# Turning q and k of three batches by DMA transposes, and spreading the value means by VectorE, in a fused attention and gated feed-forward kernel

## Chip, cores, metric

The kernel runs on one core of one Trainium2 chip. The metric is the device time of one execution in microseconds, as the median over several executions. The profile is of one more execution, recorded by the hardware profiler. Its span runs 1 to 3 us under the device time. Only fast runs are compared; a run counts as slow when it is over 1.5% above the fastest of the same kernel on its chip.

## The reference, cut to what matters

```python
B, H, S, D = 4, 8, 768, 64;  block, window = 32, 16
k_sum = k.reshape(B, H, 24, 32, D).max(axis=3)       # block maxima of the keys
v_sum = v.reshape(B, H, 24, 32, D).mean(axis=3)      # block means of the values
scores = concat(banded q k^T (|i - j| < 16), q k_sum^T + log 32)   # scaled by 1/8
x = softmax(scores) @ concat(v, v_sum)               # then (tokens, 512)
out = x + sigmoid(x w_res) * ((gelu(x w_gate) * (x w_val)) w_out)
```

Scores need q and k with the head dimension on the partitions, so q and k have to be turned. The weighted sum needs the values with the tokens on the partitions, and the block means beside them in every window.

## The kernel before

The work is cut into eight units, two per batch. An even unit of batch b and an odd one each run the feed-forward stage of 384 tokens. In the tail of each unit the attention of the next unit is computed. An odd unit also prepares the next batch in its gate/value stage. Only batch 0 is prepared ahead of all this. A **gate/value stage** is the loop of twelve `fo_step`, a **tail** is everything after it up to the next unit's first gate product, and an **odd unit** is one stage and one tail.

```python
def load_qk(src, b, parts, name):            # token p*8+j of a head -> partition p, 1 KB pieces
    ...
        nc.gpsimd.dma_start(out=t[...].rearrange("p h j d -> p h (j d)"),
                            in_=src[b, ...].rearrange("h (p j) d -> p h (j d)", j=PJ))

def v_loads(b):                              # 12 overlapping windows of 96 tokens, 128-byte pieces
    for t in range(NT):
        r0, r1, src = v_window(b, t)
        nc.gpsimd.dma_start(out=vext[b % 2][r0:r1, t, :, 0:D], in_=src)

def turn_pair(src, hp, pool, tag):           # 16 small TensorE transposes
    ...
def k_step(b, hp, pool, tag):
    tp = turn_pair(k_sb[b], hp, pool, tag)
    nc.scalar.copy(kw[:, 1:NT - 1, 0:BAND]..., src)         # ScalarE copies the windows
    nc.vector.tensor_copy(...); nc.vector.tensor_copy(...)  # VectorE the two edges
    nc.vector.tensor_reduce(out=ks..., in_=kw[...], axis=X, op=ALU.max)
    nc.vector.tensor_copy(kw[:, :, BAND:BAND + NB], ks.unsqueeze(1).to_broadcast([128, NT, NB]))

def vsum_grp(b, pool, tag):                  # block means: 12 matmuls, one copy, four small DMAs
    ...
    nc.vector.tensor_copy(vpart[:], vs[:])
    for g in range(4):
        nc.sync.dma_start(out=vsum[b % 2][96 + 6 * g:102 + 6 * g, :], in_=vpart[32 * g:32 * g + 6, :])

def vsum_bc(b, lo, hi, eng):                 # the means spread to windows lo..hi
    eng.tensor_copy(vext[b % 2][96:128, lo:hi, :, 0:D], <vsum broadcast>)

def fo_step(st, gvT, fo):                    # 8 matmuls, gelu on ScalarE, product on VectorE
    ...
    nc.scalar.activation(ge[:], g[:, 0:TU], AF.Gelu)
    nc.vector.tensor_mul(gvT[:, fo, :], ge[:], vv[:, 0:TU])   # frees vv's PSUM bank (4 banks)
...
for u in range(NU):
    b, half = u // 2, u % 2
    nb = b + 1
    if half == 0 and nb < B:
        k_sb[nb] = load_qk(k, nb, 1, "k_sb"); q_sb[nb] = load_qk(q, nb, 1, "q_sb"); v_loads(nb)
    for fo in range(FO):
        fo_step(st, gvT, fo)
        if half == 1 and nb < B:
            if fo == 1:
                vsum_grp(nb, ps_t, "t")
                vsum_bc(nb, 0, 4, nc.gpsimd); vsum_bc(nb, 4, 8, nc.gpsimd); vsum_bc(nb, 8, NT, nc.gpsimd)
            elif 2 <= fo < 6:  k_step(nb, fo - 2, ps_t, "t")
            elif 6 <= fo < 10: q_step(nb, fo - 6, ps_t, "t")
    ...                                      # tail: scores, weighted sums, residual gate, output
```

Each engine runs its instructions in program order. GpSimd issues all loads, SyncE the outputs and the small means DMAs.

The softmax here doesn't subtract the row's maximum and nothing guards it: scores larger than these inputs give would overflow.

## Time and profile before

| kernel before | value |
|---|---|
| device time, median | 306.96 us (305.46 to 307.67) |
| span of the profiled run | 304.4 us |
| PE busy | 272.4 us, 89% |
| odd units (stage + tail) of batches 1, 2, 3 being prepared | 42.4, 39.3, 38.0 us |
| even units in between | 29.7, 29.8 us |

The unit times are differences of the starts of the first gate product of each unit in the timeline.

From the page of the kernel before: the busy times, the packet count, and the chain of waits (its share of the span by engine).

```profile
PE 272.4 (89%) x2563; PEld 149.6 (49%) x2586; DVE 170.5 (56%) x375; ACT 137.7 (45%) x204; POOL 80.4 (26%) x104
...
DMA packets 54987, 22.88 MB, mean 75 GB/s; under 512 B 37480, under 2 KB 51888, under 8 KB 54960
...
PE 65%; DMA 14%; POOL 7%; DVE 6%; issue 5%; ACT 1%; POOLq 0%; DVEq 0%
```

The kernel is bound by TensorE, with 32 us in which TensorE is idle.

The timeline shows one source of it: while GpSimd spreads the means (5.57 us), VectorE's copy of the block maxima, 0.23 us at its best, takes up to 1.91 us, and the product that frees PSUM stands behind it. The GpSimd lines also show the order: the next batch's loads are issued only after the spread.

```profile
145.29 5.57 POOL L222 COPY vext_107<-vsum_109 32x2048 bf16<-32x2048 bf16 x3 [47.45 <-DMA vsum_109<-vpart]
...
149.06 1.91 DVE L192 COPY kW_2_93<-ks 128x288 bf16<-128x288 bf16 x1
...
150.81 0.77 POOL L82 DMA_DIRECT2D k_sb<-in_k_dram  x1
150.88 0.53 DVE L282 TENSOR_TENSOR gvT<-ge,vv 128x384 bf16<-128x384 f32 x1
```

### The profile page before, as it was taken

Reading aid. Unit: us, or ns where it says so; the run is one execution under the profiler, and the core shown is the slowest. Engines: PE = TensorE matmul, PEld = TensorE weight load, DVE = VectorE, ACT = ScalarE, POOL = GpSimd, SP = SyncE. Lnnn points to the kernel's source line nnn. Section 1 sums busy time; section 2 is a strip of 40 time slices with the busy share of each in tenths; the row PEclk is TensorE's granted clock in tenths of the full one; section 3 lists DMA queues with packets and bytes.
Section 4 is the critical chain, followed back from the end, with each engine's and each line's share of the span. In section 5 each row is a group of like instructions: output and inputs, shape, how many; then the busy total and the mean of one; then the engine's idle time right before and its main releaser. Section 6 shows DMA issues by size and latency. Waiting matters only on the chain.

```text
span 304.4 us, 6192 instructions
## 1 busy us (share of the span) xinstructions
PE 272.4 (89%) x2563; PEld 149.6 (49%) x2586; DVE 170.5 (56%) x375; ACT 137.7 (45%) x204; POOL 80.4 (26%) x104
## 2 busy tenths in 40 slices
PE   1665999988699999999799999999799999999993
PEld 0622565544354566455355556455354556455641
DVE  3445544673953854476933854386944854475433
ACT  2642536432466533644456533643566433643310
POOL 7976673320954000000974000000700000000000
PEclk9999599997999999999979999999999999999999
DMA  6999999991199910011099910011000110010001
GB/s 100 168 98 186 197 206 207 162 164 33 10 200 114 84 61 2 0 71 37 3 176 131 90 69 2 2 51 56 4 2 0 56 49 2 1 71 34 2 34 69
DMA packets 54987, 22.88 MB, mean 75 GB/s; under 512 B 37480, under 2 KB 51888, under 8 KB 54960
## 3 DMA queue, kind: packets, MB, share of 16 engines
q0 software_dynamic: 51360, 16.13, 81.3%
q1 hardware_dynamic: 3600, 6.37, 6.3%
q8 instruction: 20, 0.33, 0.4%
q14 instruction: 7, 0.06, 0.1%
HBM read 32.24 MB, written 6.29 MB: 127 GB/s over the span
## 4 chain that ended last, share of the span: by engine, by line
PE 65%; DMA 14%; POOL 7%; DVE 6%; issue 5%; ACT 1%; POOLq 0%; DVEq 0%
PE f L298 18%; PE g L274 16%; PE vv L278 15%; DMA vext_108<-in_v_dram 8%; PE r L288 6%; DMA w_val<-in_moe_w_val_dram 3%; DVE ks L188 3%; DMA vext_107<-in_v_dram 3%; PE tp L172 3%; PE ao L250 2%; POOL vext_107 L97 2%; PE s L232 2%; PE xp L261 2%; DVE gvT L282 2%; POOL vext_107 L222 1%
## 5 line engine op out<-in xcount | busy, mean ns | idle before, releaser
L282 DVE TENSOR_TENSOR gvT<-ge,vv 128x384 bf16<-128x384 f32 x96 | 52.9, 551 | 63.3 <-PE vv L278 63.2
L274 PE MATMUL g<-xT,w_gate 128*128 128x384 bf16 x384 | 82.3, 334 | 0.0
L281 ACT ACTIVATE ge<-g 128x384 f32<-128x384 f32 x96 | 47.1, 491 | 75.9 <-DVE gvT L282 41.3
L278 PE MATMUL vv<-xT,w_val 128*128 128x384 bf16 x384 | 80.1, 332 | 0.0
L298 PE MATMUL f<-w_out,gvT 128*128 128x512 bf16 x274 | 65.3, 379 | 1.5 <-issue 1.1
L278 PEld LDWEIGHTS <-w_val 128*128 128x128 bf16 x384 | 38.2, 100 | 26.9 <-issue 3.2
L274 PEld LDWEIGHTS <-w_gate 128*128 128x128 bf16 x384 | 35.7, 99 | 25.2 <-issue 4.2
L236 ACT ACTIVATE P<-s,bias_t 128x768 bf16<-128x768 f32 x32 | 28.9, 903 | 35.0 <-PE s L232 35.0
L298 PEld LDWEIGHTS <-gvT 128*128 128x128 bf16 x288 | 27.3, 98 | 31.0
L239 DVE TENSOR_TENSOR P<-P,maskt 128x768 bf16<-128x768 bf16 x32 | 17.7, 554 | 22.0 <-ACT P L236 22.0
L222 POOL COPY vext_108<-vsum_110 32x2048 bf16<-32x2048 bf16 x6 | 11.1, 1895 | 58.5 <-DMA vsum_110<-vpart 58.5
L288 PE MATMUL r<-w_res,xT 128*128 128x512 bf16 x88 | 24.4, 381 | 0.4
L97 POOL DMA_DIRECT2D vext_108<-in_v_dram x24 | 18.2, 770 | 18.9 <-DMA w_out<-in_moe_w_out_dram 4.7
L222 POOL COPY vext_107<-vsum_109 32x2048 bf16<-32x2048 bf16 (+1 forms) x4 | 8.3, 2108 | 47.5 <-DMA vsum_109<-vpart 47.4
L303 DVE SCALAR_TENSOR_TENSOR th<-th,f 128x512 f32<-128x512 f32 x24 | 16.3, 680 | 7.0 <-PE f L298 7.0
L97 POOL DMA_DIRECT2D vext_107<-in_v_dram x24 | 18.1, 762 | 6.5 <-PE g L274 3.3
L172 PE MATMUL tp<-ident,k_sb 96*64 96x96 bf16 x256 | 10.1, 232 | 10.6 <-DMA k_sb<-in_k_dram 6.5
L256 DVE TENSOR_TENSOR xn<-ao,rz 128x384 bf16<-128x384 f32 x32 | 17.9, 558 | 1.1
L291 ACT ACTIVATE th<-r 128x512 f32<-128x512 f32 x24 | 14.3, 594 | 8.8 <-PE r L288 8.4
L305 DVE SCALAR_TENSOR_TENSOR o<-th,xn 128x512 f32<-128x512 f32 x24 | 16.6, 692 | 0.8
L172 PE MATMUL tp<-ident,q_sb 96*64 96x96 bf16 x256 | 10.1, 232 | 6.7 <-DMA q_sb<-in_q_dram 3.0
L250 PEld LDWEIGHTS <-P 128*64 128x64 bf16 x384 | 8.9, 113 | 14.4 <-DVE P L239 5.9
(151 smaller groups left out, 220.2 us busy)
## 6 DMA issues: line engine op xcount, KB each, us to landing
out_dram<-o SPq DMA_DIRECT2D x24, 256.0 KB
k_sb<-in_k_dram POOLq DMA_DIRECT2D x3, 768.0 KB, 7.5
q_sb<-in_q_dram POOLq DMA_DIRECT2D x3, 768.0 KB, 10.6
vext_107<-in_v_dram POOLq DMA_DIRECT2D x20, 96.0 KB, 7.8
vext_108<-in_v_dram POOLq DMA_DIRECT2D x20, 96.0 KB, 10.9
w_gate<-in_moe_w_gate_dram POOLq DMA_DIRECT2D x6, 256.0 KB, 8.8
w_val<-in_moe_w_val_dram POOLq DMA_DIRECT2D x6, 256.0 KB, 9.3
w_out<-in_moe_w_out_dram POOLq DMA_DIRECT2D x3, 512.0 KB, 14.2
```

Of the source, the lines that this page charges most:

```text
L97: nc.gpsimd.dma_start(out=vext[b % 2][r0:r1, t, :, 0:D], in_=src)
L172: nc.tensor.transpose(tp[hh * 64:hh * 64 + 64, j, :], src[:, 2 * hp + hh, j, :], ident[0:PP, 0:PP])
L222: eng.tensor_copy(vext[b % 2][96:128, lo:hi, :, 0:D], src)
L236: nc.scalar.activation(P.rearrange("p a t q -> p a (t q)"), s[:, :, 0:TU], AF.Exp, scale=scale, bias=bias_t[:])
L239: nc.vector.tensor_mul(Pf, Pf, maskt.unsqueeze(1).to_broadcast([128, 2 * HT, QT]))
L256: nc.vector.tensor_mul(xn, ao[:, :, :, 0:D], rz.to_broadcast([128, NSUB, 2, D]))
L274: nc.tensor.matmul(g[:, 0:TU], w_gate[:, ko, fs], st["xT"][:, ko, :], start=(ko == 0), stop=(ko == KO - 1))
L278: nc.tensor.matmul(vv[:, 0:TU], w_val[:, ko, fs], st["xT"][:, ko, :], start=(ko == 0), stop=(ko == KO - 1))
L281: nc.scalar.activation(ge[:], g[:, 0:TU], AF.Gelu)
L282: nc.vector.tensor_mul(gvT[:, fo, :], ge[:], vv[:, 0:TU])
L288: nc.tensor.matmul(r[:], st["xT"][:, ko, ss], w_res[:, ko, :], start=(ko == 0), stop=(ko == KO - 1))
L298: nc.tensor.matmul(st["f"][:], gvT[:, fo, ss], w_out[:, fo, :], start=(fo == 0), stop=(fo == FO - 1))
```

## The change

The intent is to take q's and k's turning off TensorE, ScalarE and VectorE for batches 1 to 3. Their tokens are loaded with tokens on the partitions, and one DMA transpose each turns all of k and all of q. Values are loaded first. The means are spread by VectorE in four pieces, after the gate/value products 4 to 7, and the block maxima follow products 8 to 11.

```diff
+    k_nat = const.tile([BAND, NT, DM], BF16, name="k_nat")
+    q_nat = const.tile([128, NQ, DM], BF16, name="q_nat")
+    def load_nat(b):                       # 12 windows of k, 6 blocks of q, 128-byte pieces
+        for t in range(NT): ... nc.gpsimd.dma_start(out=k_nat[r0:r0 + hi - lo, t]..., in_=k[b, :, lo:hi, :]...)
+        for c in range(NQ): ... nc.gpsimd.dma_start(out=q_nat[:, c]..., in_=q[b, ...]...)
+
+    def turn_all(b):
+        nc.sync.dma_start_transpose(out=kW[b % 2].rearrange("d t g k -> d (t g) k")[:, :, 0:BAND],
+                                    in_=k_nat.rearrange("p t f -> p (t f)"))
+        nc.sync.dma_start_transpose(out=qT[b % 2].rearrange("d c g k -> d (c g) k"),
+                                    in_=q_nat.rearrange("p c f -> p (c f)"))
 ... (kW and qT become one tile per batch parity; k_blocks = the maxima part of k_step)
             if half == 0 and nb < B:
-                k_sb[nb] = load_qk(k, nb, 1, "k_sb")
-                q_sb[nb] = load_qk(q, nb, 1, "q_sb")
                 v_loads(nb)
+                load_nat(nb)
 ...
                     if fo == 1:
                         vsum_grp(nb, ps_t, "t")
-                        vsum_bc(nb, 0, 4, nc.gpsimd)
-                        vsum_bc(nb, 4, 8, nc.gpsimd)
-                        vsum_bc(nb, 8, NT, nc.gpsimd)
-                    elif 2 <= fo < 2 + NP:
-                        k_step(nb, fo - 2, ps_t, "t")
-                    elif 2 + NP <= fo < 2 + 2 * NP:
-                        q_step(nb, fo - 2 - NP, ps_t, "t")
+                    elif 4 <= fo < 8:
+                        vsum_bc(nb, 3 * (fo - 4), 3 * (fo - 3), nc.vector)
+                    elif 8 <= fo:
+                        k_blocks(nb, fo - 8)
 ...
             end_step(u, st, 2)
+            if half == 0 and nb < B:
+                turn_all(nb)
```

More of the change, by code (lines that the diff above doesn't have):

```diff
@@ L46 @@
     BAND = QT + 2 * WIN
+    NQ = S // 128
     PJ = 8
@@ L51 @@
     wpool = ctx.enter_context(tc.tile_pool(name="wpool", bufs=1))
-    qk = ctx.enter_context(tc.tile_pool(name="qk", bufs=2))
+    qk = ctx.enter_context(tc.tile_pool(name="qk", bufs=1))
     work = ctx.enter_context(tc.tile_pool(name="work", bufs=3))
@@ L67 @@
     warm = const.tile([128, 512], BF16, name="warm")
-    kW = [[const.tile([128, NT, 128], BF16, name=f"kW{i}_{p}") for p in range(NP)] for i in range(2)]
-    qT = [[const.tile([128, S], BF16, name=f"qT{i}_{p}") for p in range(NP)] for i in range(2)]
+    kW = [const.tile([128, NT, NP, 128], BF16, name=f"kW{i}") for i in range(2)]
+    qT = [const.tile([128, NQ, NP, 128], BF16, name=f"qT{i}") for i in range(2)]
+    k_nat = const.tile([BAND, NT, DM], BF16, name="k_nat")
+    q_nat = const.tile([128, NQ, DM], BF16, name="q_nat")
     vext = [const.tile([128, NT, H, D + 1], BF16, name=f"vext{i}") for i in range(2)]
@@ L99 @@
     k_sb, q_sb = {}, {}
+    def load_nat(b):
+        for t in range(NT):
+            lo, hi = max(0, t * QT - WIN), min(S, t * QT + QT + WIN)
+            r0 = lo - (t * QT - WIN)
+            nc.gpsimd.dma_start(out=k_nat[r0:r0 + hi - lo, t].rearrange("p (h d) -> p h d", d=D),
+                                in_=k[b, :, lo:hi, :].rearrange("h p d -> p h d"))
+        for c in range(NQ):
+            nc.gpsimd.dma_start(out=q_nat[:, c].rearrange("p (h d) -> p h d", d=D),
+                                in_=q[b, :, c * 128:(c + 1) * 128, :].rearrange("h p d -> p h d"))
+    def turn_all(b):
[3 more added lines that the diff above has]
+                                    in_=q_nat.rearrange("p c f -> p (c f)"))
     with tc.manual_schedule():
@@ L148 @@
         for p in range(NP):
-            nc.vector.memset(kW[0][p][:, 0, 0:WIN], 0.0)
-            nc.vector.memset(kW[0][p][:, NT - 1, BAND - WIN:BAND], 0.0)
-            nc.vector.memset(kW[0][p][:, :, BAND + NB:128], 0.0)
+            nc.vector.memset(kW[0][:, 0, p, 0:WIN], 0.0)
+            nc.vector.memset(kW[0][:, NT - 1, p, BAND - WIN:BAND], 0.0)
+            nc.vector.memset(kW[0][:, :, p, BAND + NB:128], 0.0)
         nc.vector.memset(warm[:], 0.0)
@@ L174, in turn_pair, with k_blocks @@
             return tp
+        def k_blocks(b, hp):
+            kw = kW[b % 2][:, :, hp]
+            ks = work.tile([128, NB], BF16, tag="ks", name="ks")
+            nc.vector.tensor_reduce(
+                out=ks.rearrange("d (t n) -> d t n", n=2),
+                in_=kw[:, :, WIN:WIN + QT].rearrange("d t (n w) -> d t n w", w=BLK),
+                axis=mybir.AxisListType.X, op=ALU.max)
+            nc.vector.tensor_copy(kw[:, :, BAND:BAND + NB], ks.unsqueeze(1).to_broadcast([128, NT, NB]))
         def k_step(b, hp, pool, tag):
             tp = turn_pair(k_sb[b], hp, pool, tag)
-            kw = kW[b % 2][hp]
+            kw = kW[b % 2][:, :, hp]
             src = bass.AP(tensor=tp.tensor, offset=tp[:, 0, 6:7].offset,
@@ L186, in k_step @@
                                   tp[:, :, PP - 10:PP].rearrange("d j p -> d p j"))
-            ks = work.tile([128, NB], BF16, tag="ks", name="ks")
-            nc.vector.tensor_reduce(
-                out=ks.rearrange("d (t n) -> d t n", n=2),
-                in_=kw[:, :, WIN:WIN + QT].rearrange("d t (n w) -> d t n w", w=BLK),
-                axis=mybir.AxisListType.X, op=ALU.max)
-            nc.vector.tensor_copy(kw[:, :, BAND:BAND + NB], ks.unsqueeze(1).to_broadcast([128, NT, NB]))
+            k_blocks(b, hp)
         def q_step(b, hp, pool, tag):
             tp = turn_pair(q_sb[b], hp, pool, tag)
-            nc.scalar.copy(qT[b % 2][hp].rearrange("d (p j) -> d p j", j=PJ),
-                           tp.rearrange("d j p -> d p j"))
+            nc.scalar.copy(qT[b % 2][:, :, hp].rearrange("d c (p j) -> d c p j", j=PJ),
+                           tp.rearrange("d j (c p) -> d c p j", c=NQ))
         def vsum_mm(b, pool, tag):
@@ L226, in s_step @@
             s = ps_s.tile([128, 2, 512], F32, tag="s", name="s")
-            kw, qt = kW[b % 2][hp], qT[b % 2][hp]
+            kw, qt = kW[b % 2], qT[b % 2]
             for t in range(HT):
@@ L231, in s_step @@
                     ps = slice(hh * 64, hh * 64 + 64)
-                    nc.tensor.matmul(s[:, hh, t * QT:(t + 1) * QT], kw[ps, tt, :],
-                                     qt[ps, tt * QT:(tt + 1) * QT], start=True, stop=True,
+                    nc.tensor.matmul(s[:, hh, t * QT:(t + 1) * QT], kw[ps, tt, hp, :],
+                                     qt[ps, tt // 2, hp, (tt % 2) * QT:(tt % 2 + 1) * QT], start=True, stop=True,
                                      skip_group_check=True)
@@ L334 @@
         own_keys(bgrp, 3)
+        nc.vector.memset(k_nat[0:32, 0], 0.0)
+        nc.vector.memset(k_nat[64:96, NT - 1], 0.0)
         for p in range(NP):
-            nc.vector.memset(kW[1][p][:, 0, 0:WIN], 0.0)
-            nc.vector.memset(kW[1][p][:, NT - 1, BAND - WIN:BAND], 0.0)
-            nc.vector.memset(kW[1][p][:, :, BAND + NB:128], 0.0)
+            nc.vector.memset(kW[1][:, 0, p, 0:WIN], 0.0)
+            nc.vector.memset(kW[1][:, NT - 1, p, BAND - WIN:BAND], 0.0)
+            nc.vector.memset(kW[1][:, :, p, BAND + NB:128], 0.0)
         for u in range(NU):
```

## The prediction

> **What bounds the kernel now.** The page gives PE 272.4 of 304.4 us; the chain of waits is PE 65%, DMA 14%. By windows, the gate/value stage of an even unit (107 to 124 us) is 17.0 us with PE busy throughout; in an odd unit, which also prepares the next batch, it is 25.7 us (136.6 to 162.3) and 25.2 (205.8 to 231). The first one (64.4 to 93) is 28.6: the timeline shows PE waiting for the last value windows until 70.0. So preparation costs about 8 us three times, plus some 3 us once. In the timeline it is 128 small transposes (8 bursts of about 0.53 us), their PSUM waits behind ScalarE's 0.96 us copies, and VectorE's 0.95 us maxima and 0.23 to 1.9 us copies, the slow ones beside GpSimd's 1.9 us copies.
>
> **Removed.** Per batch: those transposes, 8 ScalarE copies (0.8 and 0.96), 8 edge copies (0.23), GpSimd's 5.6 us of spreading. **Added.** VectorE spreads four pieces, an estimate of 0.5 us each (its 32x3072 copy took 0.96). Left on VectorE in the stage: 12 x 0.55 + 0.7 + 2 + 4 x 1.25 = about 14 us, under PE's 16 to 17. If nothing waited, an odd stage would fall to about 17.5, the time to about 280.
>
> **What I expect instead: new waits.**
> 1. Packets. q and k came in 1 KB pieces: 1,536 per batch in about 7.4 us (208 per us in the trace). Token-major they are 128-byte pieces like v's, k with overlapping windows: 8,960 + 6,144, at v's rate (about 790 per us) some 19 us; with v 31 us a batch instead of 19.
> 2. Batch 1. Weights hold the DMA until about 50 us; then v to 62, k to 73, q to 81 or later. The transposes stand on SyncE in front of the four small block-mean DMAs, and its instructions go in order. VectorE reaches the first spread at about 72, and blocks, with gate/value products behind it, until q has landed, both transposes and the small DMAs are done: 85 to 97. About 10 us of VectorE work remain then. This stage ends near 95.5 at best, more likely 103 to 106, against 93.
> 3. Batches 2 and 3 have their data early, but transposes are issued only as the odd unit begins, and VectorE needs the means about 7 us later. Transposing 1.97 MB: the Trainium skill (Advanced Engine Details and Errata, X-Bar Transpose (TRN2)) expects 350 to 400 GB/s, an estimate of 5 to 6 us; as 7,680 rows of 256 bytes at v's packet rate it is about 10 us. No record of before shows a transpose. For batch 2 the v loads of batch 3 start at the same moment and compete (11 us of DMA). I estimate the means at 12 to 20 us for batch 2, 10 to 16 for batch 3: stages of 23 to 31 and 21 to 27 against 25.
>
> **Sum.** Against before: batch 1 +10, batch 2 +3, batch 3 -2: 307 + 11 = 318 us. Range 298 to 350, skewed up because the transposes' speed is unmeasured. Faster by over 2%: 0.18; within 2%: 0.24; slower by over 2%: 0.58.
>
> **Signs.** PE loses 384 transposes; its busy time falls by some 15 us, its idle time rises by more. VectorE's first spread waits for the block-mean DMA, longest in batch 1 (12 to 25 us), and SyncE's queue waits there for q's load. DMA packets under 512 B grow by about 45,000. Even units stay near 17 us, tails near 13.
>
> **Wrong if:** transposes take 5 us, even beside loads, with SyncE free at once: then 295 to 305. Transposes or their issue over 20 us per batch: 350 or more. Or q's and k's small packets go well faster than v's, so batch 1 hardly waits.

## More of the kernel before

The kernel before scattered from 300.8 to 309.6 us over all chips used.

The next lines are stretches of the kernel before: the stage of each of the three odd units. The columns are the stretch, its length, the busy time of PE, PEld, DVE, ACT and POOL, the granted clock, the mean DMA share and GB/s. (The DMA share adds up the times of packets that overlap, so it can exceed 1.)

```profile
64.50:93.00 28.50, 23.68 (x239) 12.57 (x235) 17.32 (x32) 12.43 (x21) 12.56 (x13) 0.94 0.86 99
136.60:162.10 25.50, 23.18 (x240) 12.56 (x237) 16.39 (x32) 12.46 (x21) 12.38 (x12) 0.93 0.54 83
205.70:229.80 24.10, 21.58 (x239) 11.93 (x236) 16.48 (x32) 12.36 (x21) 5.57 (x3) 1.00 0.05 16
```

An even unit's stage takes about 16 us. So the preparation inside an odd stage costs 8 to 10 us, and 12.6 in the first. All tails are 13.8 to 13.9 us.

## The result, and the profile after

The changed kernel takes 328.85 us in the median (328.32 to 330.35) against 307.31 of the kernel before on the same chip: a ratio of 1.0713, 95% interval 1.066 to 1.0766, slower. Ratios here are the mean time of one kernel's fast runs over the mean of the other's in the same rounds, so they are not quite the ratios of the medians quoted.

From the page of the changed kernel, the lines that answer to those of before.

```profile
PE 263.6 (80%) x2202; PEld 142.6 (43%) x2202; DVE 170.2 (52%) x365; ACT 118.2 (36%) x180; POOL 102.5 (31%) x143
...
DMA packets 119689, 29.82 MB, mean 91 GB/s; under 512 B 106792, under 2 KB 116592, under 8 KB 119664
...
PE 75%; DMA 10%; SPq 6%; ACT 3%; DVE 3%; issue 2%; POOL 1%; DVEq 0%; POOLq 0%
```

SyncE's queue (SPq) is new on the chain. Stages of the three odd units of the changed kernel (the tails, 13.8 to 14.4 us, are left out):

```profile
63.50:109.10 45.60, 19.61 (x112) 10.30 (x109) 13.79 (x23) 5.90 (x13) 32.60 (x42) 0.70 2.22 157
152.80:184.00 31.20, 19.78 (x111) 10.24 (x108) 14.01 (x24) 5.91 (x13) 16.79 (x22) 0.78 1.70 161
227.60:253.00 25.40, 19.02 (x111) 10.05 (x108) 13.27 (x22) 5.88 (x12) 0.00 (x0) 0.87 0.50 92
```

TensorE's work in a stage did fall, from about 23 to 19.5 us, and ScalarE's from 12.4 to 5.9. But the stages grew from 28.5, 25.5 and 24.1 us to 45.6, 31.2 and 25.4. With the tails the odd units take 59.5, 45.0 and 39.8 us: 17.1, 5.7 and 1.8 more than before. Their sum is 24.6, the spans differ by 24.0. So the loss is wholly in these three units.

What happens in the first one is told by SyncE's timeline and by VectorE's and TensorE's (start, duration, instruction; in brackets the idle time before it and what ended it). First SyncE of the changed kernel:

```profile
72.63 9.36 SPq L115 DMA_TRANSPOSE kW_92<-k_nat  x1
82.21 8.70 SPq L117 DMA_TRANSPOSE qT_94<-q_nat  x1
90.97 2.97 SPq L239 DMA_DIRECT2D vsum_100<-vpart  x4
...
155.47 8.09 SPq L115 DMA_TRANSPOSE kW_91<-k_nat  x1
163.84 3.72 SPq L117 DMA_TRANSPOSE qT_93<-q_nat  x1
167.68 2.85 SPq L239 DMA_DIRECT2D vsum_99<-vpart  x4
...
230.28 5.95 SPq L115 DMA_TRANSPOSE kW_92<-k_nat  x1
236.46 4.20 SPq L117 DMA_TRANSPOSE qT_94<-q_nat  x1
240.76 2.85 SPq L239 DMA_DIRECT2D vsum_100<-vpart  x4
```

Then VectorE and TensorE of the changed kernel in the first odd unit:

```profile
71.38 0.55 DVE L305 TENSOR_TENSOR gvT<-ge,vv 128x384 bf16<-128x384 f32 x1 [0.75 <-PE vv L301]
100.30 0.95 DVE L245 COPY vext_98<-vsum_100 32x1536 bf16<-32x1536 bf16 x1 [28.37 <-DMA vsum_100<-vpart]
```

```profile
75.10 0.81 PE L297 MATMUL g<-xT,w_gate 128*128 128x384 bf16 x4
101.90 1.44 PE L301 MATMUL vv<-xT,w_val 128*128 128x384 bf16 x4 [25.98 <-DVE gvT L305]
103.13 1.49 PE L297 MATMUL g<-xT,w_gate 128*128 128x384 bf16 x4
```

The chain is complete in these lines. SyncE issues k's transpose at 72.6 us, when k's last window has landed, and q's behind it. (q had landed at 77.1 us by the trace; its transpose waited for SyncE, which k's held until 82.0.) Only then, at 91.0, come the four small means DMAs, whose data was ready at about 68. VectorE has reached the first spread at 71.9 and sits 28.4 us. The products behind it don't free PSUM banks, so TensorE, after filling what was free, sits 26.0 us. Afterwards four matmuls start 1.23 to 1.28 us apart group by group instead of 0.65, until 107 us, where the granted clock is back. The Trainium skill ("TensorE: Matmul & The Clock Gate", section "What's actually happening") says that the array falls to half its clock after idling and regains it with sustained work. The mean granted clock of this stage is 0.70, and about 5 us run at half speed (101.9 to 107.2).

The means landed 36.8 us after the start of the first odd unit, 22.2 after that of the second, 17.2 after that of the third. VectorE wants them after about 8.4. In the last one no load runs, and the transposes alone do it: 5.95 and 4.20 us of SyncE, and 4 us for the means. In the first the same two take 9.36 and 8.70 us, and the means another 9.3. Why, the page doesn't say, but GpSimd's timeline shows that it issued twelve v loads of batch 2 from 72.6 to 88.8 us, during these transposes, and k loads of batch 3 from 165.5 us, into the wait for batch 2's means:

```profile
72.64 6.20 POOL L100 DMA_DIRECT2D vext_97<-in_v_dram  x8
...
165.54 9.04 POOL L108 DMA_DIRECT2D k_nat<-in_k_dram  x12 [10.25 <-DMA kW_91<-k_nat]
```

### The profile page after: what moved, and what is told of

Same layout as the page of the kernel before. It is cut to its first block, busy times and chain, and to the rows that moved or that the text cites. A ratio compares the mean times of both kernels' runs of the same rounds, so it can differ in the third digit from the quotient of the medians.

```text
span 328.4 us, 5481 instructions
## 1 busy us (share of the span) xinstructions
PE 263.6 (80%) x2202; PEld 142.6 (43%) x2202; DVE 170.2 (52%) x365; ACT 118.2 (36%) x180; POOL 102.5 (31%) x143
## 2 busy tenths in 40 slices
DMA packets 119689, 29.82 MB, mean 91 GB/s; under 512 B 106792, under 2 KB 116592, under 8 KB 119664
## 4 chain that ended last, share of the span: by engine, by line
PE 75%; DMA 10%; SPq 6%; ACT 3%; DVE 3%; issue 2%; POOL 1%; DVEq 0%; POOLq 0%
PE g L297 19%; PE vv L301 19%; PE f L321 18%; PE r L311 6%; DMA vext_97<-in_v_dram 4%; SPq L117 4%; PE ao L273 3%; DMA vsum_100<-vpart 3%; PE s L255 3%; PE xp L284 2%; DMA q_sb<-in_q_dram 2%; SPq L239 2%; DMA vsum_99<-vpart 2%; PE wp L342 1%; ACT qT_93 L219 1%
## 5 line engine op out<-in xcount | busy, mean ns | idle before, releaser
L301 PE MATMUL vv<-xT,w_val 128*128 128x384 bf16 x384 | 83.0, 341 | 43.8 <-DVE gvT L305 43.8
L297 PE MATMUL g<-xT,w_gate 128*128 128x384 bf16 x384 | 84.1, 340 | 0.0
L301 PEld LDWEIGHTS <-w_val 128*128 128x128 bf16 x384 | 38.9, 101 | 72.9 <-issue 50.4
L321 PE MATMUL f<-w_out,gvT 128*128 128x512 bf16 x288 | 68.4, 379 | 0.0
L297 PEld LDWEIGHTS <-w_gate 128*128 128x128 bf16 x384 | 38.5, 102 | 29.0 <-issue 8.2
L108 POOL DMA_DIRECT2D k_nat<-in_k_dram x36 | 27.2, 762 | 16.6 <-DMA kW_91<-k_nat 10.3
L245 DVE COPY vext_98<-vsum_100 32x1536 bf16<-32x1536 bf16 x8 | 7.6, 952 | 37.3 <-DMA vsum_100<-vpart 37.1
L262 DVE TENSOR_TENSOR P<-P,maskt 128x768 bf16<-128x768 bf16 x32 | 17.7, 553 | 16.8 <-ACT P L259 16.8
L100 POOL DMA_DIRECT2D vext_97<-in_v_dram x24 | 18.3, 784 | 7.3 <-DMA vext_97<-in_v_dram 6.5
L328 DVE SCALAR_TENSOR_TENSOR o<-th,xn 128x512 f32<-128x512 f32 x24 | 16.6, 692 | 0.8
L111 POOL DMA_DIRECT2D q_nat<-in_q_dram x18 | 15.8, 911 | 0.0
L277 DVE RECIPROCAL rz<-ao 128x6 f32<-128x6 f32 x32 | 6.2, 193 | 12.8 <-PE ao L273 12.8
## 6 DMA issues: line engine op xcount, KB each, us to landing
w_out<-in_moe_w_out_dram POOLq DMA_DIRECT2D x3, 512.0 KB, 13.8
```

The lines of the kernel that those rows point to most:

```text
L108: nc.gpsimd.dma_start(out=k_nat[r0:r0 + hi - lo, t].rearrange("p (h d) -> p h d", d=D), in_=k[b, :, lo:hi, :].rearrange("h p d -> p h d"))
L262: nc.vector.tensor_mul(Pf, Pf, maskt.unsqueeze(1).to_broadcast([128, 2 * HT, QT]))
L297: nc.tensor.matmul(g[:, 0:TU], w_gate[:, ko, fs], st["xT"][:, ko, :], start=(ko == 0), stop=(ko == KO - 1))
L301: nc.tensor.matmul(vv[:, 0:TU], w_val[:, ko, fs], st["xT"][:, ko, :], start=(ko == 0), stop=(ko == KO - 1))
L321: nc.tensor.matmul(st["f"][:], gvT[:, fo, ss], w_out[:, fo, :], start=(fo == 0), stop=(fo == FO - 1))
```

## The experiments

Theory A: the time is lost by order. VectorE waits, in order, for means that stand behind the transposes on SyncE. Theory A' is named in e4's expectation ("Theory A with contention") and tested by itself in e6, after the first four runs: A, and the waits are as long as they are because GpSimd's loads run ahead and compete with the transposes. Rival B: the small packets of q and k cost the time, wherever the transposes stand. Rival C: VectorE has too much work in the stage. All diffs are against the changed kernel unless said otherwise. All results below but one (e3, wrong in its values) compute the reference's result.

The table gives each odd unit's time in the profile (from its first gate product to that of the next unit), the median, and the ratio to the kernel before of the same rounds.

| run | odd units, us | median, us | ratio (95%) |
|---|---|---|---|
| before | 42.4, 39.3, 38.0 | 305.1 to 307.3 | 1 |
| changed | 59.5, 45.0, 39.8 | 328.85 | 1.0713 (1.066 to 1.0766) |
| e1 means first | 51.2, 35.7, 35.5 | 307.60 | 1.0087 (1.0048 to 1.0127) |
| e2 means by ScalarE | 51.5, 36.7, 36.6 | 310.24 | 1.0166 (1.0123 to 1.0209) |
| e3 no q and k loads | 43.7, 41.2, 39.7 | 311.93 | 1.0232 (1.0206 to 1.0258) |
| e4 spread by GpSimd | 39.4, 32.9, 34.7 | 293.08 | 0.9612 (0.957 to 0.9654) |
| e5 other part alone | 41.1, 36.9, 36.9 | 302.18 | 0.99 (0.9875 to 0.9926) |
| e6 GpSimd waits | 47.6, 39.8, 39.4 | 312.25 | 1.0311 (1.0187 to 1.0434) |
| e7 early transposes | 60.0, 34.7, 31.3 | 311.15 | 1.0276 (1.0113 to 1.044) |
| e8 e4 + early transposes | 39.2, 30.6, 30.6 | 285.31 | 0.9425 (0.9316 to 0.9534) |
| e9 e8, batch 1 on TensorE | 39.6, 30.6, 30.7 | 286.83 | 0.9474 (0.9364 to 0.9584) |
| e10 e11, two spreads | 46.1, 30.7, 30.6 | 295.02 | 0.9659 (0.9631 to 0.9688) |
| e11 e6 + early transposes | 42.9, 31.6, 31.4 | 296.12 | 0.9695 (0.967 to 0.972) |
| e12 e8, batch 1's means first | 43.7, 30.6, 30.7 | 290.72 | 0.9509 (0.9465 to 0.9554) |

e1 to e4, e6 to e9, and e10 to e12 with e5 shared a chip and its runs of the kernel before each time. The medians of before on these three chips lie within 0.7 us, so medians are set side by side across them.

The recorded verdicts, at 2% and from fast runs alone: changed and e3 slower; e1 and e5 the same; e4, e10, e11 and e12 faster; e2 and e6 to e9 unclear. For e6 to e9 the three fast runs of before are 305.1, 304.8 and 300.8 us, and the last one widens the interval. Against the mean of all seven, 305.1 us, their ratios would be 1.023, 1.020, 0.935 and 0.940.

### e1: the means DMAs ahead of the transposes

```diff
                         vsum_grp(nb, ps_t, "t")
+                        turn_all(nb)
 ...
-            if half == 0 and nb < B:
-                turn_all(nb)
```

> The changed kernel, with both transposes issued after the four block-mean DMAs on SyncE (in the odd unit, right after the group sums) instead of before them. Theory A (the time is lost because the block-mean DMAs stand behind the transposes in SyncE's order, and VectorE, which waits for the means in order, holds back the gate/value products): VectorE's first spread comes about 8.5 us after the odd unit's start in all three batches, its wait there is under 2 us; the later transposes then delay the block maxima and the next scores instead. Odd gate/value stages of about 30 (batch 1, data late), 23 and 20 us; about 303 us in all. Rival B (the 45,000 more small DMA packets of q and k cost the time wherever the transposes stand): still 320 us or more. Rival C (VectorE has too much work in the odd stage): unchanged within 5 us, 324 or more.

Measured: 307.60 us, ratio 1.0087. VectorE's first spread in batch 1:

```profile
74.80 0.95 DVE L245 COPY vext<-vsum 32x1536 bf16<-32x1536 bf16 x1 [2.97 <-DMA vsum<-vpart]
```

It waits 3.0 us there and 0.4 in batch 2, and the loss of the change is all but gone, as A says; B and C are 12 us or more off. A's figure of 303 was too low by 5 us. The first stage took 35.0 us, not 30: k's transpose took 9.66 us and q's 10.29, VectorE waited 8.9 us for the first maxima and TensorE 5.3 us for q. That pointed to the transposes being slow in batch 1 whatever stands behind them. GpSimd's v loads of batch 2 ran beside them here too, from 72.2 us.

### e2: the means DMAs issued by ScalarE

```diff
-            nc.sync.dma_start(out=vsum[b % 2]...
+            nc.scalar.dma_start(out=vsum[b % 2]...
```

> The changed kernel, with the four block-mean DMAs issued by ScalarE instead of SyncE; the transposes stay where they are. Theory A: the means no longer stand behind the transposes, VectorE's first spread comes about 9 us after the odd unit's start; batch 1 is still held by the late q and k (next scores at about 94 us instead of 109), batches 2 and 3 have stages of 18 to 19 us against 31 and 25; in all about 294 us, faster than the kernel before. ScalarE loses some 3 us per batch to issuing. Rival B (small packets): 320 or more. Rival C (VectorE's work): 324 or more.

Measured: 310.24 us, a miss by 16 us in its size, though again far under B and C. In batch 2 the first spread comes 13.9 us after the odd unit's start, not 9. ScalarE's and SyncE's lines of this run in the second odd unit say where it went:

```profile
147.09 8.21 SPq L115 DMA_TRANSPOSE kW<-k_nat  x1
149.04 5.19 ACTq L239 DMA_DIRECT2D vsum<-vpart  x4
154.33 0.87 ACT L304 ACTIVATE ge<-g 128x384 f32<-128x384 f32 x2 [7.08 <-DMA vsum<-vpart]
```

The four issues take ScalarE 5.19 us beside a transpose's issue, where the first odd unit's four, issued before any transpose, took 3.38. The gelu behind them waits 7.08 us, and with it the product and TensorE. A second queue didn't get the small DMAs past the transposes cheaply. What makes the issue slow is not shown.

### e3: q and k of batches 1 to 3 not loaded (wrong result on purpose)

```diff
                 v_loads(nb)
-                load_nat(nb)
 ...
-        nc.vector.memset(k_nat[0:32, 0], 0.0)
-        nc.vector.memset(k_nat[64:96, NT - 1], 0.0)
+        nc.vector.memset(k_nat[:], 0.0)
+        nc.vector.memset(q_nat[:], 0.0)
```

> Wrong result on purpose: q and k of batches 1 to 3 are not loaded (their tiles are zeroed once), the rest of the changed kernel is kept, so 45,000 small packets less and no wait for data. Theory A: only batch 1 gains, its transposes start at about 66 us instead of 72.6 and end sooner; the stages are 29 to 31, 31 and 25 us instead of 45, 31 and 25; 314 us in all (311 to 319). Rival B (the packets of q and k are the cost): back at the time of before or under it, 290 to 307. Rival C: 325 or more.

Measured: 311.93 us, within A's 311 to 319. With 45,312 fewer small load packets the kernel is still 2.3% slower than before, so B can't be the whole. The first odd unit gained 15.8 us. The second gained 3.8, which A had not expected: in the changed kernel k's and q's loads of batch 3 start when batch 2's k transpose ends (165.5 us) and share the DMA engines with q's transpose and the means, which then landed 7.3 us after their first issue instead of 4.1 here. The loads matter, then, through what they collide with.

### e4: the means spread by GpSimd, as before the change

```diff
                         vsum_grp(nb, ps_t, "t")
-                    elif 4 <= fo < 8:
-                        vsum_bc(nb, 3 * (fo - 4), 3 * (fo - 3), nc.vector)
+                        vsum_bc(nb, 0, 4, nc.gpsimd)
+                        vsum_bc(nb, 4, 8, nc.gpsimd)
+                        vsum_bc(nb, 8, NT, nc.gpsimd)
```

> The changed kernel, with the means spread by GpSimd in three pieces as before, the DMAs and transposes as changed. VectorE no longer waits for the means, and GpSimd, waiting for them in its order, issues the next batch's v loads only afterwards, so they do not compete with the transposes. Theory A with contention: the means land at about 90 us instead of 100 in batch 1, and 17 us after the odd unit's start in batches 2 and 3 (22 and 17 before); each transpose pair takes 6 + 4 us on SyncE; the values weighted by the scores wait for the spread by some 4 us; about 292 to 300 us in all. If competing loads are not what slows the transposes of batch 1 (9.4 and 8.7 us), these stay near 9 us. Rival B: 320 or more.

Measured: 293.08 us, 3.9% faster than the kernel before, in the expected 292 to 300. Every packet and both transposes of the change are still there, in the same order on SyncE. Means landed at 88.7 us instead of 100.3, and the transposes of batch 1 took SyncE 7.53 and 4.79 us instead of 9.36 and 8.70. So B falls. But this run changes two things at once: VectorE no longer blocks, and GpSimd's loads no longer run ahead. e6 parts them.

### e6: VectorE's spread kept, GpSimd made to wait for the means

```diff
+    hold = const.tile([128, 1], BF16, name="hold")
 ...
                         vsum_grp(nb, ps_t, "t")
+                        nc.gpsimd.tensor_copy(hold[96:128, :], vsum[nb % 2][96:128, 0:1])
```

> The changed kernel in everything, and in addition GpSimd copies one column of the means (32 elements) in the odd unit, so that it issues the next batch's loads only after the means have landed. VectorE still spreads and still waits behind the transposes. Theory A' (the prediction's mechanism is right and its size was off because GpSimd runs ahead with the next batch's loads, which slow the transposes and the small means DMAs in batches 1 and 2): the first spread comes at about 89 us instead of 100 in batch 1 and 17 to 18 us after the odd unit's start instead of 22 in batch 2, as in the run with GpSimd's spread; batch 3 is unchanged at 17; about 312 us in all, 16 less. If competing loads do not matter: 326 or more.

Measured: 312.25 us, as expected to 0.3 us. This is the run that shows why the loss was larger than predicted. One copy of 0.19 us on GpSimd takes 16.6 us off the medians (328.85 to 312.25) and 18.3 off the spans. These are not of the same rounds; the ratios to before, 1.0713 and 1.0311, give some 12 us, the second with an interval of 4 us to either side. SyncE and GpSimd of this run in the first odd unit, and VectorE's first spread in the second:

```profile
71.59 7.55 SPq L116 DMA_TRANSPOSE kW<-k_nat  x1
79.37 3.64 SPq L118 DMA_TRANSPOSE qT<-q_nat  x1
83.07 2.98 SPq L240 DMA_DIRECT2D vsum<-vpart  x4
```

```profile
87.24 0.19 POOL L379 COPY hold<-vsum 32x1 bf16<-32x1 bf16 x1 [15.42 <-DMA vsum<-vpart]
87.77 9.18 POOL L101 DMA_DIRECT2D vext<-in_v_dram  x12 [0.34 <-issue]
...
156.73 0.95 DVE L246 COPY vext<-vsum 32x1536 bf16<-32x1536 bf16 x1 [8.41 <-DMA vsum<-vpart]
```

Batch 2's v loads now start at 87.8 instead of 72.6 us, and the first spread comes at 87.2 instead of 100.3. The packet records tell it directly. A batch's transposes write 7,680 packets of 256 bytes. In the changed kernel's batch 1 these were spread over 20.5 us, with 9,061 packets of 128 bytes of loads in between them; here over 10.0 us, with 775. In the changed kernel's batch 3, where no load runs, it was 10.4 us. The Trainium skill ("DMA: Bandwidth & Descriptors", section "Issuing engines are not separate DMA queues") says that DMAs of all issuing engines run on the same 16 DMA engines and interleave. The price of it was a factor of two.

### e7: transposes of batches 2 and 3 issued an even unit earlier

```diff
                 v_loads(nb)
                 load_nat(nb)
+                if nb > 1:
+                    turn_all(nb)
 ...
-            if half == 0 and nb < B:
+            if half == 0 and nb == 1:
                 turn_all(nb)
```

> The changed kernel with the transposes of batches 2 and 3 issued at the start of the even unit instead of its end; batch 1 and VectorE's spread as changed. Theory A: in batches 2 and 3 the means come 8.5 to 9 us after the odd unit's start and VectorE hardly waits; gate/value stages of 18 us instead of 31 and 25, tails of 14; batch 1 unchanged at 45; about 308 us in all. Rival C (VectorE's four spreads at 0.95 us and four maxima are themselves too long for the stage): stages of 21 us or more, 315 or more.

Measured: 311.15 us. With the transposes out of the way the last two stages fell from 31.2 and 25.4 us to 20.7 and 17.2, batch 1 stayed at 60.0 for its unit. A is right and C falls: the stage with all of VectorE's new work fits in 17.2 us. Batch 2's 20.7 was to be 18; its first spread waited 3.6 us, because k's loads of batch 3 were under way and the means landed 7.4 us after their first issue.

### e8: e4 and e7 together

The edit is the two diffs of those runs, and nothing else.

> The kernel of the run with GpSimd's spread, with the transposes of batches 2 and 3 issued at the start of the even unit. Batch 1 as in that run (39 us for the odd unit), batches 2 and 3 with a stage of 17 and a tail of 14 us instead of 17 and 16 to 18, since the means come early and the spread ends before the weighted values need it: about 287 us in all, 6 less than that run.

Measured: 285.31 us, ratio 0.9425 (0.9316 to 0.9534): the fastest of all, 4.7 to 6.8% under the kernel before by that interval. Its four runs lie between 285.2 and 285.8 us, and the lowest of the seven of before on that chip is 300.8. The stages and tails of its three odd units:

```profile
62.80:85.60 22.80, 17.61 (x112) 9.60 (x110) 11.07 (x21) 7.17 (x13) 8.84 (x11) 0.93 1.74 183
85.60:102.00 16.40, 15.76 (x157) 7.71 (x157) 10.42 (x24) 6.68 (x8) 14.12 (x14) 0.89 0.93 60
131.70:148.50 16.80, 16.80 (x113) 9.45 (x111) 10.62 (x20) 5.93 (x13) 8.04 (x7) 1.00 0.29 71
148.50:162.30 13.80, 13.80 (x157) 7.01 (x157) 10.89 (x24) 7.80 (x9) 13.22 (x18) 1.00 3.18 123
192.10:208.90 16.80, 16.80 (x115) 9.45 (x113) 10.65 (x21) 5.97 (x13) 5.57 (x3) 1.00 0.06 22
208.90:222.70 13.80, 13.80 (x158) 7.02 (x158) 10.63 (x23) 7.77 (x9) 0.00 (x0) 1.00 0.09 34
```

In batches 2 and 3 TensorE is busy through the whole unit, 30.6 us, hardly more than an even unit. It has as many small DMA packets as the changed kernel (119,690 and 119,689). What remains is batch 1, whose data can't be there in time: 39.2 us.

### e9: in e8, batch 1's q and k loaded in 1 KB pieces and turned on TensorE

```diff
-                load_nat(nb)
-                if nb > 1:
-                    turn_all(nb)
+                if nb == 1:
+                    k_sb[nb] = load_qk(k, nb, 1, "k_sb"); q_sb[nb] = load_qk(q, nb, 1, "q_sb")
+                else:
+                    load_nat(nb); turn_all(nb)
 ... (k_step and q_step for nb == 1, k_blocks for the others; no turn_all at the end of the even unit)
```

> As the run with early transposes and GpSimd's spread, but batch 1 gets q and k in 1 KB pieces after the values and turns them on TensorE as the kernel before does; only batches 2 and 3 are transposed by DMA. Theory A: batch 1's odd unit takes about 38.5 us (stage 24.5, tail 14) against 39.4; batches 2 and 3 about 31 each as there; about 286 us in all, and the best of all. If the late data of batch 1 were no cost of its own, it would be slower than that run by the 8 us that TensorE's transposes cost.

Measured: 286.83 us, as expected to 1 us, but not the best: batch 1's unit takes 39.6 us against 39.2. For batch 1 the two ways of turning are worth the same within 0.4 us. What the DMA transposes save on TensorE, the late data takes.

### e11 and e10: both corrections, with VectorE's spread in four and in two pieces

e11 is e6 and e7 together. e10 is e11 with this:

```diff
-                    elif 4 <= fo < 8:
-                        vsum_bc(nb, 3 * (fo - 4), 3 * (fo - 3), nc.vector)
+                    elif fo in (4, 6):
+                        vsum_bc(nb, 3 * (fo - 4), 3 * (fo - 2), nc.vector)
```

> The changed kernel with both corrections and VectorE's spread kept: transposes of batches 2 and 3 at the start of the even unit, and GpSimd waiting for the means before the next loads. Theory: first spread at about 87 us in batch 1 and 8.5 us after the odd unit's start in batches 2 and 3; odd units of about 47, 32 and 32 us; 295 to 298 us in all, 11 to 13 more than with GpSimd's spread, nearly all of it in batch 1, where VectorE still blocks.

> As the next run (e11), but VectorE spreads in two pieces of six windows instead of four of three. In the traces so far a VectorE piece of six windows (32x3072, once, batch 0) took 0.96 to 1.01 us and one of three windows (32x1536) 0.95 us. If that holds, VectorE has 1.9 us less per batch, and the time is 2 to 4 us under that of e11; if a piece of six takes 1.9 us here, no difference over 1 us.

Measured: 296.12 us for e11, as expected, and 295.02 for e10. In e11's profile batch 1's odd unit took 42.9 us, not 47, as that execution started it some 3 us later (67.9 us) and so waited less. In batches 2 and 3 the first spread comes 8.7 us after the start and the units take 31.6 and 31.4 us. So with the order mended, VectorE's spread costs about 1 us a batch over GpSimd's there (30.6 in e8). The rest of the difference to e8 is batch 1, where VectorE blocks until 88.1 us: the unit after it starts at 110.8 us, in e8 at 102.0. e10's gain of 1.1 us is under the 2 to 4 expected, although the durations held. A piece of six windows in e10 took 0.96 us, twice the data of a piece of three:

```profile
149.27 0.96 DVE L246 COPY vext<-vsum 32x3072 bf16<-32x3072 bf16 x1 [0.32 <-DMA vsum<-vpart]
```

In the changed kernel a piece of three windows took 0.95. In batches 2 and 3 the units fell from 31.6 and 31.4 us to 30.7 and 30.6, which is all that could be gained there.

### e5: the other part of the change alone

Against the kernel before: values loaded ahead of q and k, and VectorE's spread in four pieces after products 4 to 7; q and k in 1 KB pieces and turned on TensorE as there.

```diff
+                v_loads(nb)
                 k_sb[nb] = load_qk(k, nb, 1, "k_sb")
                 q_sb[nb] = load_qk(q, nb, 1, "q_sb")
-                v_loads(nb)
 ...
-                        vsum_bc(nb, 0, 4, nc.gpsimd)
-                        vsum_bc(nb, 4, 8, nc.gpsimd)
-                        vsum_bc(nb, 8, NT, nc.gpsimd)
 ...
+                    if 4 <= fo < 8:
+                        vsum_bc(nb, 3 * (fo - 4), 3 * (fo - 3), nc.vector)
```

> The kernel before with the other part of the change alone: values loaded before k and q, and their means spread by VectorE in four pieces (after the gate/value products 4 to 7); q and k still come in 1 KB pieces and are turned on TensorE. Expected: the first odd unit no longer waits for values (stage 28.6 to about 25.5), VectorE gets 4 x 0.95 us more but its block copies are no longer slowed by GpSimd's; stages of 25 us; about 301 us in all (297 to 306). If VectorE's spread were a large part of the changed kernel's loss, 310 or more.

Measured: 302.18 us, ratio 0.99. This part of the change gains 1%; the odd units are 1.3, 2.4 and 1.1 us shorter than in the profile of before. All its sixteen copies of the block maxima took 0.23 to 0.30 us; in the kernel before the six that ran beside GpSimd's spread took 0.58 to 1.91, the other ten 0.23 to 0.57. So VectorE's spread costs nothing by itself. Nor do the DMA transposes: e4, which has them and leaves the spread to GpSimd, is 3.9% faster than before. Only the two together lose 7%: the spread then waits, in VectorE's order, for means that stand behind the transposes, and GpSimd's loads run ahead (e6).

### e12: in e8, batch 1's means DMAs ahead of its transposes

```diff
                         vsum_grp(nb, ps_t, "t")
+                        if nb == 1:
+                            turn_all(nb)
 ... (and no turn_all at the end of the even unit)
```

> The best run so far (early transposes, GpSimd's spread), with batch 1's transposes issued after its block-mean DMAs, since q and k are not there earlier anyway. The means land at about 75 us instead of 88 in batch 1, the spread ends at 81, so the tail no longer waits for it (13.9 us instead of 16.4); but batch 2's loads then start at 81 us and compete with q's transpose, which can cost 2 to 4 us of it. About 283 to 287 us in all.

Measured: 290.72 us, worse than e8's 285.31 by 5, and outside the expected 283 to 287. The means landed at 75 us as planned, so GpSimd was released at 80.6 and issued batch 2's v loads into the q transpose. In this run's TensorE timeline:

```profile
90.13 0.50 PE L255 MATMUL s<-qT,kW 64*128 64x64 bf16 x12 [4.46 <-DMA qT<-q_nat]
```

The scores waited 4.5 us for q (0.5 in e4 and e8), and the twelve output matmuls after them took 4.55 us instead of 3.46 in e8, at the lower clock. It is the collision that e6 takes away, brought back by a correction: an earlier means DMA let the loads start earlier. The packet records show where the delay sits. The last 256-byte packet of batch 1's transposes was over at 85.5 us here and at 85.1 in e8. Late were the 32 four-byte packets that follow q's transpose on SyncE's queue: they were over at 88.2 us, among load packets, and at 85.1 in e8. That these packets tell of the landing is argued, not shown.

## Why the prediction was right or wrong

- **Right: the direction, and the chain.** The prediction forecast slower and gave the reason: the transposes stand on SyncE in front of the means DMAs, VectorE blocks at the first spread at about 72 us (measured 71.9), the products behind it hold TensorE. e1 moves the means and the loss is nearly gone.
- **Right in part: the times of the data.** k was to land at 73 us (72.6 by the trace). q was to land at 81 or later and landed earlier, at 77.1; its transpose came at 82.2 all the same, because k's held SyncE until then. Small load packets were to grow by 45,000: the 128-byte ones grew from 35,840 to 81,152. All packets under 512 bytes grew by 69,312, since the 23,040 packets of the transposes were left out of the count.
- **Wrong: the size, +11 us against +21.5 in the medians.** The step that failed is "until q has landed, both transposes and the small DMAs are done: 85 to 97", with its "batch 1 +10" and, of the same cause, "I estimate the means at 12 to 20 us for batch 2". The means came at 100.3 us and after 22.2. The odd units grew by 17.1, 5.7 and 1.8 us, where +10, +3 and -2 stood. What batch 1 waited for was not q's landing. The term that was mis-sized is the time of transposes and means DMAs *beside loads*: the transposes of batch 1 took 20.5 us where the prediction had about 10, and 10.0 in e6; the means DMAs took 9.3 us from their first issue to their use, and 4.1 in e6. The prediction saw competition in batch 2 only. It missed that GpSimd, freed of the spread, issues batch 2's v loads at 72.6 us, just as batch 1's transposes begin, and batch 3's k loads at 165.5 us into the wait for batch 2's means (7.3 us from their first issue to their use, against 4.0 in batch 3). The instruction streams show that order, and it could have been read there.
- **Shown by e6.** With nothing changed but GpSimd's wait, the means come at 87.2 us and 16.8 after the odd unit's start, both within the ranges of the prediction. The loss that is left is 6 to 10 us: 6.4 by the medians of its chip, 7.1 by the odd units, about 9.5 by the ratio 1.0311. So without the collision 11 would have been near, in part by luck: the odd units grew by 5.2, 0.5 and 1.4 us, where +10, +3 and -2 stood, and the first stage ended at 95.2 us, the prediction's "at best", not at 103 to 106.
- **A smaller error, in batch 3.** No load runs there, and still it is +1.8 instead of -2. The means came after 17.2 us (10 to 16 predicted). VectorE's piece took 0.95 us, not 0.5: halving the data of the known copy did not halve its time. And the stage was compared with 25 us where the exact starts give 24.1. These are argued from the trace, not tested by themselves, but e10 shows how little the pieces' length is worth.
- **Right by one of two estimates: the transposes' own speed.** From the packet rate of the v loads the prediction had about 10 us for 7,680 rows. Where no load ran beside them they took 10.0 to 11.0 us over all runs. The skill's figure gave 5 to 6.
- **Signs that were off.** TensorE's busy time fell by 8.8 us, not 15, while its idle time doubled from 32 to 65 us; the matmuls after each wait run at half clock and so take longer. Tails stayed at 13.8 to 14.4 us and were 13.9 before, not 13. VectorE waited 28.4 us in batch 1, more than the 12 to 25 given. SyncE's queue did not wait for q's load.

What stays open: why ScalarE's DMA issues are slow beside a transpose (e2), and why VectorE's copy of three windows takes as long as one of six (e10).

## What to carry to other kernels

When a change frees an engine that issues DMAs, ask what it will now issue earlier, and what that will share the DMA engines with: a wait that cost nothing may have been the only thing keeping loads out of the way of a transfer on the critical path. Put short DMAs that someone waits for ahead of long ones on the same queue, and issue the long ones as soon as their data and their destination allow: here the kernel with all transposes issued late is 7% slower than before, and e8 is about 6% faster, with those of batches 2 and 3 issued one unit earlier and the spread back on GpSimd. With the spread left on VectorE and only GpSimd's wait restored (e11) it is 3% faster. An instruction that waits for a DMA should not stand, on an in-order engine, in front of work that frees another engine's buffers.

## What the Trainium skill lacked or had wrong

- "Advanced Engine Details and Errata", section "X-Bar Transpose (TRN2)", says that transposes are as fast as regular DMAs and expects 350 to 400 GB/s. Here the two transposes of a batch, 1.97 MB in 256-byte packets from SBUF to SBUF, took 10.0 to 11.0 us where no load ran beside them, 179 to 196 GB/s, and 20.5 us, 96 GB/s, beside loads.
- No page gives, as measured on this chip, the time that issuing one large transpose holds the queue's engine. ("DMA: Bandwidth & Descriptors" has such times in a part on trn3, with a column in cycles for "previous generations" and no size of a tile beside it; no run here tests it.) SyncE was held 5.9 to 6.3 us for k (96 x 6,144 elements) and 3.7 to 4.5 us for q (128 x 3,072) where no load ran beside them, and 9.4 and 8.7 us in the changed kernel's batch 1; instructions behind wait that long.
- "DMA: Bandwidth & Descriptors", section "Issuing engines are not separate DMA queues", is right that DMAs interleave, but says that the issue time saved by a second engine "is usually small relative to the DMA itself". It was not small for four DMAs of 6 KB: in batch 3 of the changed kernel 2.85 us of SyncE, of 4.0 us from the first issue to the use of the means. ScalarE took 3.38 us for them before any transpose and 5.19 us beside one.
- "TensorE: Matmul & The Clock Gate" agrees in the main: half speed after idling. Its section "What's actually happening" says that work of the first 3.4 us or so runs at half speed and everything after it at full speed. In the changed kernel's three odd units full speed came back 5.3, 5.7 and 4.2 us after work resumed. The section's own remark that the window runs freely fits this: in that trace the clock's changes lie whole multiples of 3.41 us apart.
